# An FFT mixer and a routed expert layer on one core: two small expert blocks taken from the first half of the first batch

## The chip, the cores and the metric

The kernel runs on one core of a Trainium2 chip. The core has a matrix engine (TensorE, "PE" in the profile, with its weight loads "PEld"), a vector engine (VectorE, "DVE"), an activation engine (ScalarE, "ACT"), a general engine (GpSimd, "POOL") and SyncE ("SP"), which here only issues DMAs. Each engine works through its own instructions strictly in the order in which the program lists them, and waits for others by semaphores. Sixteen DMA engines move data between the core's memory and DRAM. The metric is the device time of one execution in microseconds.

## The reference

The input `x` is 8 batches of 2496 rows of 256 numbers. A two-dimensional Fourier transform is taken of each batch, and its real part is kept. The 19968 rows are then routed: each row goes to one of eight experts, the one with the largest logit.

```python
X = np.fft.fft(x, axis=1)
X = np.fft.fft(X, axis=2)
x = X.real.astype(np.float32).reshape(B * S, D)
logits = x @ w_gate
expert_idx = np.argmax(logits, axis=1)
...
for e in range(E):
    h = np.maximum(x_sorted[lo:hi] @ w1[e], 0.0)
    y_sorted[lo:hi] = h @ w2[e]
return gate_w[:, None] * y
```

`w1[e]` is 256x1024 and `w2[e]` is 1024x256, so a row costs an expert 524,288 multiplications; the weights of an expert are 2 MB in float32.

## The kernel before

**The transform of a batch** has two stages. `first(b)` (line 325) loads the batch in three parts, folds them on VectorE (`fold`, lines 299 to 310), multiplies by `w1` tables (`half1`, PSUM name `s`) and stores the result to a DRAM tensor `Td`. `regroup` (line 351) loads it back in another arrangement as `t4`. `second(b)` (line 361) takes one group after the other: `turn_last` (matmul `pr`), `group` (matmul `p<-table,t`, copied by ScalarE to `zz`), and for each of ten windows of 128 positions the last matmul (`p<-table,zz`), which gives the rows and their eight logits together. The ten windows are two halves of five (`h` is 0 or 1; `HW` is 5). A window gives 2 x 128 rows, a position and its mirror image, so a half has `NSL` = 10 slots of 128 rows. 24 of the first half's rows are doubles that are thrown out: it has 1256 rows.

**The routing** is done once for each half: `route` (line 416) finds the expert of each row, counts with bf16 matmuls (`rk`) how many rows of the same expert came before, and computes each row's place in `Xs`, a DRAM tensor with a long region for every expert (line 450 to 453). `base` holds how far each region is filled. For batch 0, VectorE writes the places directly as integers to `pi` (line 453); for later batches it writes floats to `pf`.

**The scatter.** `route` appends ten entries to the queue `waiting`. Each call of `send` (line 462) takes one: for later batches ScalarE copies the slot's place to `due` and GpSimd casts it to an integer (line 469); then GpSimd issues an indirect DMA that writes 128 rows to their places in `Xs` (line 470, and 236 in the profile). Writes to `Xs` and reads of it are ordered by dependency groups that `sent` and `taken` declare (lines 241 to 249): a block that is taken in round `b` waits for all scatters up to batch `b`, and not for those of `b + 1`.

**Expert blocks.** `rounds` (line 130) plans how many blocks are taken after which batch. After batch `b`, the number of rows is known, but not how they are spread over the experts; if every expert may leave a remainder smaller than a block, a certain number of full blocks is there in any case, and only these are planned. Before the change that gives 2 blocks of 256 and 4 of 128 rows after batch 0, 4 of 256 after batch 1, 3 of 512 after batch 2, 5 of 512 after each of the later ones, and in the last round 7 of 256 and 21 of 128 in addition. Which expert each of the planned blocks belongs to and where its rows start is computed on VectorE by `plan` (line 478), some twenty small instructions on one partition, in five turns (it yields four times; the table `tabs[b, size, last]` exists after the fifth). Its tables have room for `MOST` = 21 blocks, and their instructions work on all 21 whatever the number `k` of blocks is. `gone` holds what the blocks planned so far have taken.

**A block** (`experts`, line 701) needs its rows (`fetch_rows`, line 526: SyncE reads the table, then issues four DMAs at line 534 and one at line 538), its weights (`fetch_weights`, line 541: two DMAs of 1024 KB at lines 544 and 546, into one of three buffers), a transpose on VectorE with a negation on ScalarE (`turn`, line 576), the first product `ph` with its ReLU evictions (line 792 to 798), the second product `py` (line 833) and an indirect DMA for each 128 rows of the output. `fetch_some` (line 722) asks for weights and rows of the next blocks, as far as their tables exist and their batch is in the set `whole`.

**The order of the work** is written out by generators. Ahead of the main loop, `second(0)` runs with `first(1)` interleaved, and one `send` after each of its turns (line 937 to 940); eight of batch 0's twenty scatters are called there, the other twelve in the main loop. The main loop (line 943) asks `experts` for one step of expert work at a time; each yields a weight and a flag. For every step the loop lets `side` do a number of turns: `ticks` x weight / (`EARLY` x `open_`), where `ticks` is 44 in the first round and `open_` is 32, the weight of that round's blocks. A step of weight 0 without the flag is worth one turn. `side` in the first round weaves `close(0)` (the plans of batch 0) turn by turn with batch 1's and the next transform. Before the first block, the loop makes turns until the first table exists (nine), sends everything that is still waiting when `experts` yields `0, True` (line 744, 956 to 960), and makes nine more turns (line 746) ahead of the first transpose.

Of the kernel before, what the change touches and what calls it, by code (L numbers as in the profile page):

```python
# [50 lines left out]
def bc(ap, axis, n):  # L51
    shape = list(ap.shape)
    shape.insert(axis, n)
    return ap[tuple([slice(None)] * axis + [None])].to_broadcast(shape)
# [72 lines left out]
    return {n: np.ascontiguousarray(v, dtype=np.float32) for n, v in c.items()}  # L127


def rounds():  # L130

    want = [((256, 2), (128, 4)), ((256, 4),)] + [((512, B),)] * (B - 2)
    plan, used = [], 0

    def full(done, size):
        return max(0, -(-(done - used - E * (size - 1)) // size))

    for b in range(B):  # L140
# [12 lines left out]
        plan.append(now)  # L153
    return plan

SURE = -(-(NT - sum(size * k for now in rounds() for size, k, last in now if not last)) // REST)


def in_order():


    todo = []
    for b, now in enumerate(rounds()):
        parts = [[(b, size, last, i) for i in range(k)] for size, k, last in now]
        if b == B - 1:
            few, many = parts[-2:]
            sure, more = many[:SURE], many[SURE:]
            k = len(few)  # L170
# [45 lines left out]
def kernel(ctx: ExitStack, tc, x, w_gate, w1, w2, out):  # L216
# [52 lines left out]
    con, k = {}, 0  # L269
# [91 lines left out]
    def second(b):  # L361

        t4 = None

        def turn_last(h):

            nonlocal t4
            t4 = ahead.pop((b, "t4", h))
            n = min(HALF, NG - h * HALF)
            pr = pm_.tile([GP, HALF], F32, tag="m", name="pr")  # L370
            mm(pr[:, 0:n], con["rot"][:], t4[0:GP, 0:n, H])
            act.copy(t4[0:GP, 0:n, H], pr[:, 0:n])

        def group(g):
            i, n = g % HALF, LAST if g == NG - 1 else GP
            p2 = pm_.tile([128, 2, n], F32, tag="m", name="p2")
            for c in range(2):
                mm(p2[:, c], t4[0:GP, i, c * H:(c + 1) * H], con["m2"][:, c, 0:n])
            act.copy(zz[:, :, g * GP:g * GP + n], p2[:])  # L379
            if g == HALF - 1:  # L380
                turn_last(1)

        def mirror(rows, k):
            act.copy(free(rows[:], (k + 1) * W + D - 1, [-W, 2], [-1, H - 1]),
                     free(rows[:], k * W + 1, [W, 2], [1, H - 1]))

        turn_last(0)
        yield
        group(0)
        yield  # L390
        group(1)
        yield
        for h in range(2):
            rows = sp.tile([128, NSL, W], F32, tag="rows", name="rows")
            lg = sp.tile([128, NSL, E], F32, tag="lg", name="lg")
            for i in range(HW):
                w, k = HW * h + i, 2 * i
                if w + 2 < NG:
                    group(w + 2)
                p3 = pm_.tile([128, 2 * NY + 2 * E + 1], F32, tag="m", name="p3")  # L400
                z = zz[:, :, 128 * w:128 * (w + 1)]
                mm(p3[:, 0:NY + 2 * E], z[:, 0], con["rd"][:, 0, 0:NY + 2 * E], True, False, skip_group_check=True)
                mm(p3[:, NY:], z[:, 1], con["rd"][:, 1], False, True, skip_group_check=True)
                zs = sp.tile([128, NY + 1], F32, tag="zs", name="zs")
                act.copy(zs[:], p3[:, NY + 2 * E:])  # L405
                if i:
                    mirror(rows, k - 2)
                vec.tensor_copy(lg[:, k:k + 2], p3[:, NY:NY + 2 * E].rearrange("p (m e) -> p m e", m=2))  # L408
                for m, op in enumerate((ALU.add, ALU.subtract)):
                    vec.scalar_tensor_tensor(rows[:, k + m, 0:NY], p3[:, 0:NY], zs[:, 0:1], zs[:, 1:],  # L410
                                             op0=ALU.add, op1=op)
                yield
            mirror(rows, k)
            yield from route(b, h, rows, lg)

    def route(b, h, rows, lg):
# [33 lines left out]
        vec.tensor_tensor(pos[:], rk[:, 0:NSL], bc(base[:], 1, NSL), op=ALU.add)  # L450
        vec.tensor_tensor(pos[:], pos[:], oh[:, 0:NSL], op=ALU.mult)
        vec.reduce_sum(pf[:], pos[:], axis=AX_X)
        vec.tensor_tensor(pf[:] if b else pi[:], pf[:], con["far"][:, h], op=ALU.add)
        nxt = cp.tile([128, E], F32, tag="base", name="base", bufs=2)
        vec.tensor_tensor(nxt[:], rk[:, NSL], base[:], op=ALU.add)
        base = nxt
        for s in range(NSL):
            waiting.append((b, pf[:, s:s + 1], pi[:, s:s + 1], rows[:, s]))

    waiting = deque()  # L460

    def send():

        if waiting:
            b, place, idx, rows = waiting.popleft()
            if b:
                due = sp.tile([128, 1], F32, tag="due", name="due", bufs=8)
                act.copy(due[:], place)  # L468
                pool.tensor_copy(idx, due[:])  # L469
            sent(put_row(Xs, idx, rows, E * CAP - 1, "xs"), b)  # L470


# [5 lines left out]
    def plan(b, size, k, last):  # L478
# [3 lines left out]
        def one(name, *dims, dt=F32):  # L482
            return cp.tile([1, *dims], dt, tag="p_" + name, name="p_" + name, bufs=2)
# [10 lines left out]
        vec.tensor_tensor(ex[:], ce[:], nb[:], op=ALU.subtract)  # L494
        yield
        vec.scalar_tensor_tensor(rb[:], ex[:], -float(size), gone[:], op0=ALU.mult, op1=ALU.add)
        ge, ei = one("ge", MOST, E), one("ei", MOST)
        val, eq, rw = one("val", MOST, E + 1), one("eq", MOST, E + 1), one("rw", MOST)
        vec.tensor_tensor(ge[:], bc(bk["i"], 2, E), bc(ce[:], 1, MOST), op=ALU.is_ge)
        vec.reduce_sum(ei[:], ge[:], axis=AX_X)  # L500
        yield
        vec.tensor_tensor(eq[:], bc(ei[:], 2, E + 1), bc(bk["e9"], 1, MOST), op=ALU.is_equal)
        vec.memset(val[:, :, E:E + 1], float(E * CAP))
        vec.scalar_tensor_tensor(val[:, :, 0:E], bc(bk["i"], 2, E), float(size), bc(rb[:], 1, MOST),
                                 op0=ALU.mult, op1=ALU.add)
        yield
        vec.tensor_tensor(val[:], val[:], eq[:], op=ALU.mult)
        vec.reduce_sum(rw[:], val[:], axis=AX_X)
        tab = cp.tile([1, 2, MOST], I32, tag="p_tab", name="p_tab", bufs=4)
        vec.tensor_copy(tab[:, 0], rw[:])  # L510
        vec.tensor_scalar(tab[:, 1], ei[:], E - 1.0, None, op0=ALU.min)
        if last:
            cnt = cp.tile([1, 1], I32, name="cnt")
            vec.tensor_copy(cnt[:], ce[:, E - 1:E])
# [186 lines left out]
    def experts(todo):  # L701
# [35 lines left out]
        for k, (b, size, last, at) in enumerate(todo):  # L737
            n, m = size // 128, BIG // size
            if not k:
                while todo[0][:3] not in tabs:  # L740
                    yield 0, False
                fetch_some(0, 1)
                while b not in whole:
                    yield 0, True
                fetch_some(0)
                for _ in range(9):
                    yield 0, False
                for xT in turn(b, size, xbs[0][0]):
                    pass
# [114 lines left out]

    def close(b):

        for size, k, last in rounds()[b]:
            yield from plan(b, size, k, last)

    def through(b):  # L870
# [5 lines left out]
    def ahead_of(b):  # L876

        yield from first(b)
        regroup(b, 0)
        regroup(b, 1)  # L880
# [43 lines left out]
    for c in range(2):  # L924
# [6 lines left out]
            vec.tensor_scalar(con["rd"][:, c, to + E:to + 2 * E], pg[:], con["sgn"][:], None, op0=ALU.mult)  # L931
        else:
            vec.tensor_copy(con["rd"][:, c, to + E:to + 2 * E], pg[:])
    early = ahead_of(1)
    for _ in range(7):
        next(early)
    for k, _ in enumerate(second(0)):
# [5 lines left out]
    for b in range(1, B):  # L943
# [3 lines left out]
        ticks = TICKS + AHEAD * (b == 1)  # L947
        if b == 1:
            side = woven(chain(close(0), through(0)), chain(early, side))
        blocks = [(size, k * size / BIG, halved(b - 1, size)) for size, k, _ in rounds()[b - 1]]  # L950
# [76 lines left out]
```

## Time and profile before

| | us |
|---|---|
| median of 3 runs | 1272.84 (1270.5 to 1274.08) |
| profiled execution | 1280.92 |
| its span, first to last instruction | 1279.1 |
| TensorE busy / mean granted clock | 1221.0 (95%) / 0.972 |
| VectorE, ScalarE, GpSimd busy | 700.4 (55%), 436.3 (34%), 398.3 (31%) |
| indirect DMA to `Xs`, GpSimd, mean of one | 1.02 |
| cast of 128 places on GpSimd, mean of one | 0.28 |

In the lists of the profile a line has the start, the duration, the engine, the source line, the operation and its tiles, then how often in a row, and in brackets how long the engine was idle before it and who ended that. Every float32 matmul of the program stands as two records (`x8` is four matmuls). Ends of matmuls are modelled. "remote" stands where the trace doesn't tell what ended a wait. Line 221 is the helper through which all matmuls go, line 236 that of all indirect DMAs.

### The profile page before, as it was taken

The page shows a single profiled execution, that of the slowest core. Times are in us where ns is not written, and L with a number is a line of the kernel's source. Part 1 is how long each engine was busy: PE and PEld are TensorE (multiplying, and loading weights), DVE is VectorE, ACT ScalarE, POOL GpSimd, SP SyncE. Part 2 cuts the span into 40 slices and gives each one's busy share as a digit, 9 for nine tenths or more (in the row PEclk, how much of TensorE's full clock was granted, in tenths as well). Part 3 has the DMA queues.
Part 4 walks back from the last instruction along what each step waited for, and adds up shares of the span by engine and source line. Part 5 has one row for each costly group of instructions (what it writes and reads, how often), then busy time and mean ns, then how long its engine had stood idle before and what let it go on. Part 6 is the DMA issues. An engine that isn't in the chain of part 4 may idle for free.

```text
span 1279.1 us, 21208 instructions
## 1 busy us (share of the span) xinstructions
PE 1221.0 (95%) x6905; PEld 1077.0 (84%) x6905; DVE 700.4 (55%) x1772; ACT 436.3 (34%) x1096; POOL 398.3 (31%) x495
## 2 busy tenths in 40 slices
PE   6768999999999999999999999999999999999996
PEld 4557898876788888888888888888889999999995
DVE  4455434343466655564556455674578774444662
ACT  1423332332243433434343343432333332222232
POOL 0235327145116311561116411461453321111112
PEclk6859999999999999999999999999999999999998
DMA  8859798765348553573336434443435238778786
GB/s 241 279 181 321 242 339 297 204 228 175 125 146 260 162 153 113 175 240 114 104 118 211 144 120 149 132 152 107 130 121 167 91 129 296 283 277 276 280 279 246
DMA packets 163211, 249.72 MB, mean 195 GB/s; under 512 B 118601, under 2 KB 130227, under 8 KB 143516
## 3 DMA queue, kind: packets, MB, share of 16 engines
q1 hardware_dynamic: 146327, 203.28, 50.0%
q0 software_dynamic: 15888, 42.14, 9.1%
q10 hardware_dynamic: 885, 2.94, 0.7%
q8 instruction: 56, 0.92, 0.3%
q14 instruction: 55, 0.45, 0.1%
HBM read 194.91 MB, written 54.83 MB: 195 GB/s over the span
## 4 chain that ended last, share of the span: by engine, by line
PE 87%; DMA 6%; DVE 3%; another core or an unknown queue 2%; issue 1%; ACT 1%; SPq 0%; POOL 0%; POOLq 0%; DVEq 0%; ACTq 0%
PE py L221 32%; PE ph L221 10%; PE c L221 10%; PE a L221 10%; PE p L221 6%; PE d L221 6%; PE b L221 5%; PE e L221 4%; PE s L221 3%; DMA xq<-in_x_dram 2%; DMA Td<-t 1%; DMA t<-Td 1%; DMA xb<-Xs 1%; PE rk L221 0%
## 5 line engine op out<-in xcount | busy, mean ns | idle before, releaser
L221 PE MATMUL py<-w_sb,hT 128*128 128x256 f32 x2016 | 454.9, 380 | 1.3 <-DVE hT L796 1.3
L221 PEld LDWEIGHTS py<-w_sb,hT 128*128 128x128 f32 x2016 | 377.6, 190 | 51.2 <-DVE hT L796 1.7
L236 POOL DMA_INDIRECT out_dram<-y,ro x163 | 160.4, 984 | 694.0 <-ACT y L837 482.6
L236 POOL DMA_INDIRECT Xs<-rows,pi x160 | 163.2, 1020 | 109.9 <-DVE rows L410 52.1
L221 PE MATMUL ph<-xT,w_sb 128*128 128x128 f32 (+2 forms) x992 | 171.3, 328 | 6.1 <-DVE hT L796 3.3
L221 PEld LDWEIGHTS ph<-xT,w_sb 128*128 128x128 f32 x992 | 135.5, 192 | 30.5 <-issue 17.9
L837 ACT ACTIVATE y<-py,xb 128x256 f32<-128x256 f32 x129 | 61.0, 473 | 239.5 <-PE py L221 213.0
L221 PE MATMUL a<-xT,w_sb 128*128 128x256 f32 (+1 forms) x512 | 117.5, 356 | 0.0
L621 DVE TENSOR_TENSOR u<-p,b 128x512 f32<-128x512 f32 x57 | 39.1, 687 | 124.2 <-PE b L221 95.0
L796 DVE TENSOR_SCALAR hT<-ph 128x512 f32<-128x512 f32 x43 | 29.7, 690 | 129.5 <-issue 79.2
L221 PEld LDWEIGHTS a<-xT,w_sb 128*128 128x128 f32 x512 | 89.5, 190 | 10.7 <-DVE xT L582 0.4
L408 DVE COPY lg<-p 128x16 f32<-128x16 f32 x80 | 13.9, 174 | 141.5 <-ACT zs L405 121.3
L631 ACT ACTIVATE hT<-a 128x512 f32<-128x512 f32 x57 | 34.0, 597 | 149.5 <-PE a L221 115.7
L585 ACT ACTIVATE xT<-xT 128x256 f32<-128x256 f32 (+1 forms) x94 | 36.4, 387 | 121.8 <-DVE xT L582 71.9
L221 PE MATMUL s<-xq,w 104*112 104x256 f32 (+2 forms) x208 | 62.6, 426 | 11.0 <-DVE xq L297 10.9
L221 PEld LDWEIGHTS p<-table,t 120*128 120x128 f32 x352 | 55.2, 206 | 15.0 <-ACT zz L379 5.5
L221 PE MATMUL p<-table,zz 128*128 128x145 f32 (+1 forms) x320 | 57.2, 304 | 7.6 <-ACT t L321 5.5
L221 PE MATMUL p<-table,t 120*128 120x120 f32 (+1 forms) x352 | 57.7, 291 | 6.1 <-ACT zz L379 4.1
L221 PE MATMUL c<-xT,ws 128*128 128x256 f32 (+1 forms) x256 | 59.5, 359 | 3.2 <-DVE hT L627 3.2
L469 POOL CAST pi<-due 128x1 int32<-128x1 f32 x140 | 39.5, 282 | 69.1 <-ACT due L468 68.7
L582 DVE STREAM_TRANSPOSE xT<-xb 128x512 f32<-128x512 f32 (+1 forms) x94 | 58.2, 625 | 4.3 <-DMA xb<-Xs 4.3
L798 ACT ACTIVATE hT<-ph 128x512 f32<-128x512 f32 x55 | 32.8, 597 | 80.2 <-PE ph L221 64.9
(146 smaller groups left out, 1798.1 us busy)
## 6 DMA issues: line engine op xcount, KB each, us to landing
w_sb<-in_moe_w_dram SPq DMA_DIRECT2D x132, 1024.0 KB
xq<-in_x_dram SPq DMA_DIRECT2D x24, 896.0 KB
xb<-Xs SPq DMA_DIRECT2D x112, 128.0 KB
Td<-t SPq DMA_DIRECT2D x18, 448.0 KB
t<-Td SPq DMA_DIRECT2D x8, 768.0 KB
t<-Td SPq DMA_DIRECT2D x8, 640.0 KB
xb<-Xs SPq DMA_DIRECT2D x52, 64.0 KB
xb<-Xs SPq DMA_DIRECT2D x100, 32.0 KB
```

Source lines behind the costliest of these rows:

```text
L221: nc.tensor.matmul(o, lhsT=lhsT, rhs=rhs, start=start, stop=stop, **kw)
L236: return unordered(pool.indirect_dma_start(out=dst, out_offset=bass.IndirectOffsetOnAxis(ap=idx, axis=0), in_=rows, in_offset=None, bounds ...
L408: vec.tensor_copy(lg[:, k:k + 2], p3[:, NY:NY + 2 * E].rearrange("p (m e) -> p m e", m=2))
L469: pool.tensor_copy(idx, due[:])
L582: vec.transpose(free(xT[:], 256 * h, [32, n // 32], [BIG, 2], [1, 32]), free(xb, 512 * h, [64, n // 32], [1, 2], [2, 32]))
L585: act.activation(odd, odd, ACTF.Copy, scale=-1.0)
L621: vec.tensor_tensor(u2[:], p1[:], b[:], op=add)
L631: act.activation(h11, a[:], ACTF.Relu)
L796: vec.tensor_scalar(o, ph[:], 0.0, None, op0=ALU.max)
L798: act.activation(o, ph[:], ACTF.Relu)
L837: act.activation(y[:], py[:], ACTF.Copy, scale=meta[:, i, 1:2])
```

## The change

A new first stage, called batch -1 and named `HEAD`, holds two blocks of 128 rows that can be planned after the first half of batch 0. `rounds` counts their 256 rows as taken, so that batch 0's own list becomes one block of 256 and four of 128; the other rounds' lists stay as they were.

- The plan of these blocks, `heads = close(-1)`, takes one turn ahead of each of the five windows of batch 0's second half.
- The ten places of batch 0's first half stand in `waiting` under -1, those of its second half under 0, so their scatters are in different dependency groups.
- Batch 0's places are floats too, and GpSimd casts each slot's (from `pf` directly, without the copy by ScalarE) ahead of its scatter.
- `plan`'s instructions from line 499 on work on the `k` blocks of the plan instead of 21.
- There are eight turns of other work ahead of the first block's transpose instead of nine; the nine turns until the first table exists fall away, since the first table is there when the main loop begins.
- The main loop's first round counts the head's weight: `open_` stays 32.

```diff
+HEAD = [(REST, -(-(2 * 128 * HW - NB - E * (REST - 1)) // REST), False)]
 def rounds():
-    plan, used = [], 0
+    plan, used = [], sum(size * k for size, k, _ in HEAD)
...
+def stage(b):
+    return HEAD if b < 0 else rounds()[b]
...
 def in_order():
-    for b, now in enumerate(rounds()):
+    for b in range(-1, B):
+        now = stage(b)
...
             for i in range(HW):
+                if h and not b:
+                    next(heads, None)
...
-        vec.tensor_tensor(pf[:] if b else pi[:], pf[:], con["far"][:, h], op=ALU.add)
+        vec.tensor_tensor(pf[:], pf[:], con["far"][:, h], op=ALU.add)
...
-            waiting.append((b, pf[:, s:s + 1], pi[:, s:s + 1], rows[:, s]))
+            waiting.append((b if b or h else -1, pf[:, s:s + 1], pi[:, s:s + 1], rows[:, s]))
...
-            if b:
+            if b > 0:
                 due = sp.tile([128, 1], F32, tag="due", name="due", bufs=8)
                 act.copy(due[:], place)
-                pool.tensor_copy(idx, due[:])
+                place = due[:]
+            pool.tensor_copy(idx, place)
             sent(put_row(Xs, idx, rows, E * CAP - 1, "xs"), b)
...
-        ge, ei = one("ge", MOST, E), one("ei", MOST)
-        val, eq, rw = one("val", MOST, E + 1), one("eq", MOST, E + 1), one("rw", MOST)
-        vec.tensor_tensor(ge[:], bc(bk["i"], 2, E), bc(ce[:], 1, MOST), op=ALU.is_ge)
-        vec.reduce_sum(ei[:], ge[:], axis=AX_X)
+        ge, val, eq = (one(name, MOST, E + 1)[:, 0:k] for name in ("ge", "val", "eq"))
+        ei, rw = (one(name, MOST)[:, 0:k] for name in ("ei", "rw"))
+        count = bk["i"][:, 0:k]
+        vec.tensor_tensor(ge[:, :, 0:E], bc(count, 2, E), bc(ce[:], 1, k), op=ALU.is_ge)
+        vec.reduce_sum(ei, ge[:, :, 0:E], axis=AX_X)
...
-                for _ in range(9):
+                for _ in range(8):
                     yield 0, False
...
     def close(b):
-        for size, k, last in rounds()[b]:
+        for size, k, last in stage(b):
             yield from plan(b, size, k, last)
...
-    early = ahead_of(1)
+    heads, early = close(-1), ahead_of(1)
...
-        blocks = [... for size, k, _ in rounds()[b - 1]]
+        blocks = [... for size, k, _ in (HEAD if b == 1 else []) + stage(b - 1)]
```

More of the change, by code (lines that the diff above doesn't have):

```diff
@@ L154, in rounds @@
     return plan
-SURE = -(-(NT - sum(size * k for now in rounds() for size, k, last in now if not last)) // REST)
+def stage(b):
+    return HEAD if b < 0 else rounds()[b]
+SURE = -(-(NT - sum(size * k for now in [HEAD, *rounds()] for size, k, last in now if not last)) // REST)
 def in_order():
     todo = []
-    for b, now in enumerate(rounds()):
+    for b in range(-1, B):
+        now = stage(b)
         parts = [[(b, size, last, i) for i in range(k)] for size, k, last in now]
@@ L496, in plan @@
         vec.scalar_tensor_tensor(rb[:], ex[:], -float(size), gone[:], op0=ALU.mult, op1=ALU.add)
-        ge, ei = one("ge", MOST, E), one("ei", MOST)
-        val, eq, rw = one("val", MOST, E + 1), one("eq", MOST, E + 1), one("rw", MOST)
-        vec.tensor_tensor(ge[:], bc(bk["i"], 2, E), bc(ce[:], 1, MOST), op=ALU.is_ge)
-        vec.reduce_sum(ei[:], ge[:], axis=AX_X)
+        ge, val, eq = (one(name, MOST, E + 1)[:, 0:k] for name in ("ge", "val", "eq"))
[3 more added lines that the diff above has]
+        vec.reduce_sum(ei, ge[:, :, 0:E], axis=AX_X)
         yield
-        vec.tensor_tensor(eq[:], bc(ei[:], 2, E + 1), bc(bk["e9"], 1, MOST), op=ALU.is_equal)
+        vec.tensor_tensor(eq, bc(ei, 2, E + 1), bc(bk["e9"], 1, k), op=ALU.is_equal)
         vec.memset(val[:, :, E:E + 1], float(E * CAP))
-        vec.scalar_tensor_tensor(val[:, :, 0:E], bc(bk["i"], 2, E), float(size), bc(rb[:], 1, MOST),
+        vec.scalar_tensor_tensor(val[:, :, 0:E], bc(count, 2, E), float(size), bc(rb[:], 1, k),
                                  op0=ALU.mult, op1=ALU.add)
         yield
-        vec.tensor_tensor(val[:], val[:], eq[:], op=ALU.mult)
-        vec.reduce_sum(rw[:], val[:], axis=AX_X)
+        vec.tensor_tensor(val, val, eq, op=ALU.mult)
+        vec.reduce_sum(rw, val, axis=AX_X)
         tab = cp.tile([1, 2, MOST], I32, tag="p_tab", name="p_tab", bufs=4)
-        vec.tensor_copy(tab[:, 0], rw[:])
-        vec.tensor_scalar(tab[:, 1], ei[:], E - 1.0, None, op0=ALU.min)
+        vec.tensor_copy(tab[:, 0, 0:k], rw)
+        vec.tensor_scalar(tab[:, 1, 0:k], ei, E - 1.0, None, op0=ALU.min)
         if last:
@@ L949 @@
             side = woven(chain(close(0), through(0)), chain(early, side))
-        blocks = [(size, k * size / BIG, halved(b - 1, size)) for size, k, _ in rounds()[b - 1]]
+        blocks = [(size, k * size / BIG, halved(b - 1, size)) for size, k, _ in (HEAD if b == 1 else []) + stage(b - 1)]
         total = sum(k * (15 if seven_ else 16) for _, k, seven_ in blocks)
```

## The prediction

> **What bounds the kernel now.** I read the page's slices first, then stretches of 5 us, then the timeline around the first expert block, then SyncE's waits. The slices:
>
> ```profile
> PE   6768999999999999999999999999999999999996
> ...
> PEclk6859999999999999999999999999999999999998
> DMA  8859798765348553573336434443435238778786
> ```
>
> A slice is 32 us. From the fifth one on TensorE has work in every tenth that the row can show, at full clock; a matmul block saved or added there is time saved or added, and nothing else is. The idle time lies in the first four slices, so the change must be judged between about 52 us (first scatter) and 140 us. Stretches of 5 us, with busy time, granted clock, DMA share and GB/s:
>
> ```profile
> 60.00:65.00 5.00, 1.88 (x7) 0.50 0.85 307
> 65.00:70.00 5.00, 1.48 (x7) 0.50 0.22 78
> 70.00:75.00 5.00, 3.69 (x11) 0.50 0.69 189
> 75.00:80.00 5.00, 1.21 (x4) 0.50 0.99 375
> 80.00:85.00 5.00, 3.07 (x13) 0.50 0.24 76
> 85.00:90.00 5.00, 3.25 (x15) 0.77 0.48 86
> 90.00:95.00 5.00, 4.99 (x19) 0.66 0.76 254
> ```
>
> For 30 us TensorE has batch 1's transform pieces alone, with gaps and at half clock. What it waits for is the end of batch 0's scatter and, behind it, the first block's rows:
>
> ```profile
> 52.53 1.11 POOL L236 DMA_INDIRECT Xs<-rows,pi  x1 [52.08 <-DVE rows L410]
> 53.94 0.97 POOL L236 DMA_INDIRECT Xs<-rows,pi  x1 [0.30 <-issue]
> ...
> 78.33 0.97 POOL L236 DMA_INDIRECT Xs<-rows,pi  x1 [0.31 <-issue]
> ...
> 83.46 1.92 SPq L534 DMA_DIRECT2D xb<-Xs  x4
> ...
> 90.01 3.16 PE L221 MATMUL ph<-xT,w_sb 128*128 128x256 f32 x8 [1.75 <-DVE ro L755]
> ```
>
> Twenty scatters leave GpSimd from 52.53 to 79.30; SyncE stands at line 534 until 83.46; the first expert matmul runs at 90.01.
>
> **How much TensorE loses there.** At full clock four records of `p<-table,t` take 0.43 us start to start, four of `p<-table,zz` 0.51, four of `s` 0.86. From 61.3 to 90 the timeline holds 24 + 16 + 8 of them and two `pr`s: 2.6 + 2.0 + 1.7 + 0.3 = 6.6 us of work in 30 us, 23.4 lost. From 90 to 105 there are four groups of the first block's `ph` (1.73 each, 6.9 us) and 5.8 us of transform: 2.3 lost. So 25.7 us are lost from 60 to 105, beside 6.9 us of expert work and 12.4 us of transform done.
>
> **The change, part by part.**
>
> *One 256 block becomes two of 128.* By the planner's arithmetic batch 0 had 2x256 + 4x128 rows in sure blocks; now it has 2x128 (from its first 1256 rows), 1x256, 4x128. All later rounds stay the same. The price on TensorE is read from the pure 128 blocks:
>
> ```profile
> 159.80 3.73 PE L221 MATMUL ph<-xT,w_sb 128*128 128x128 f32 x32
> 163.37 3.62 PE L221 MATMUL py<-w_sb,hT 128*128 128x256 f32 x16
> 166.83 3.73 PE L221 MATMUL ph<-xT,w_sb 128*128 128x128 f32 x32
> ```
>
> 166.83 - 159.80 = 7.03 us for a block, 14.06 for two. A 256 block is four `ph` groups of 1.73 and two `py` of 3.46, 13.83. So +0.24 us. Evictions (4), output scatters (2) and row bytes stay the same. SyncE gets two more table loads, two weight transfers of 1024 KB and five row transfers.
>
> *When the first block can start.* Its rows need only sends 1 to 10. A cast goes ahead of each: with casts, sends follow at 121.80, 123.26, 124.71, so 1.455 us against 1.275 (53.94 to 55.22). First send 52.53 + 0.20 cast + 0.28 gap = 53.0; the tenth 9 x 1.455 later, 66.1. The twentieth was issued at 78.33 and SyncE was released at 83.46, so 5.1 us to landing at most: 71.2. From SyncE's row transfer to the first matmul took 83.46 to 90.01, 6.5 us, but with nine filler turns and a 256 block in between; its own parts are 1.92 issue, 0.43 transpose, 0.31 negation, and about 1.8 of flight, an estimate from these gaps: 4.5. First matmul at 75.7 (74 to 78).
>
> *The filler is postponed.* Before, 18 turns of side work passed ahead of the first block, nine of them batch 1's; now 8, four of them batch 1's: three folds on VectorE and one `pr`. So TensorE has almost nothing from 62 to 75.7: 15.6 lost from 60. This is the bill for starting earlier; the postponed transform has to be done between the head blocks. A weighted turn of a block still draws 44 / (0.7 x 32) = 1.96 turns.
>
> *The head blocks' own losses.* Cold clock: before, TensorE came back to full clock 4.4 us after its first block started, half of which is 2.2 lost. Late completions: ScalarE waited for transform results long after the matmuls' modelled ends, while GpSimd sent without a break:
>
> ```profile
> ACT t L372 <- remote: 5.0, 1, 5.0
> ACT zz L379 <- remote: 4.8, 1, 4.8
> ACT zs L405 <- remote: 4.0, 1, 4.0
> ```
>
> These fell between 61 and 81, 13.8 us in 20; VectorE had 7.7 more at 120 to 132. GpSimd will send until about 83.5 (20 x 1.455 from 53.0, and 1.4 for two sends that took 1.77 and 1.57 instead of 0.97), so the head lies 7.8 us in this. From 0 (280 to 300 us, where sends are as dense and no such wait stands) to 5.4 (7.8 x 13.8 / 20). I take 3.
>
> *The sum.* Before lost 25.7; after loses 15.6 + 2.2 + 3.0, and does 0.24 more: 4.7 us gained. What is late next is the 256 block's rows: batch 0's last send ends at 83.5 and lands by 88.6, its rows are there by 93 to 97; the head blocks need 14.1 of their own and 11 of transform from 75.7, beyond 104. Hidden by 7 us or more.
>
> *The queues.* SyncE asks for the first head block's weights once the early table is there, about 59.5 instead of 71.19, then stands at the head's rows until 71 rather than at batch 0's until 83.46; behind it are only the second head block's rows and weights, asked for by 78 and landed by 85, needed at about 90. On GpSimd each send waits for its own cast, 20 x 0.18 = 3.6 us over all, inside the cover just named; without that cover it would be paid once.
>
> *The plans.* `heads` puts five turns of plan work on VectorE among the second half's windows: with the rows of the present plan (1.48 us from line 488 to 494, then pieces of about 0.8, 0.7 and 1.7) some 4 to 5 us at most beside 1.7 us of VectorE idling there. It delays the second half's places from 63.6 to about 66.5; send 11 would go at 67.5, so nothing is paid. Shorter plans save some 0.15 us in six VectorE instructions of each of eleven plans; TensorE covers both: 0.
>
> The Trainium skill, "TensorE: Matmul & The Clock Gate", Part 1: The HAM clock gate, says that an idle window of some 3.4 us halves the clock and as much steady work restores it. It speaks against the change, which leaves a longer gap ahead of the head; the rows of 0.50 from 60 on agree. By that page the cold start would cost 1.7 instead of 2.2, and the sum would be an estimated 5.2.
>
> "SBUF — State Buffer", SBUF: two separate sides, says that a VectorE instruction with two SBUF inputs and a GpSimd instruction that reads SBUF shut each other out. The two slow sends at 65.44 and 67.51 stand beside such folds (lines 306, 295), which agrees. The early plan's two-input steps among the first ten casts could by that page hold GpSimd up by an estimated 1.8 us, and the gain would be 2.9.
>
> **The rivals.**
>
> *The first rows come late (slower).* Place: SyncE at line 534. If the row transfer waits for all twenty sends, the last is issued at 82.1, lands at about 88.6, and the first matmul runs at 93 with the filler not done: lost 32.9 + 2.2 up to there against 25.7, so -9.6 with the extra work, 1282. Every microsecond that the head starts after 80.4 is a loss; from 84.2 on it can be measured. For it: weights asked for at 59.5 compete with sends 5 to 10 on a DMA row at 0.85. Against: the two halves are in different dependency groups, and the DMA engines stand at 0.22 from 65 to 70.
>
> *The added weights meet full DMA engines.* From 92 to 136 us they are 0.92 to 1.03 busy at 306 to 347 GB/s. 2.1 MB more at 300 are 7 us; if paid there: 1272.8 - 4.7 + 7 = 1275.1. Against: the head's first weights fall into 60 to 70, the second's into 78 to 92, where the engines are at 0.22 to 0.5.
>
> *Late completions hold both head blocks*, at 5.4 for the first and a like stall of 2 for the second: 1272.8 - 0.3 = 1272.5, no change.
>
> *A better one.* No late completions (+3), and the stall of 120 to 132 (7.3 us: 1.99 us groups at 121.09 and 126.37 with 5.3 between) half gone: about 1261.
>
> **How the numbers follow.** The profiled execution took 1280.92, its span 1279.1, and is 8.1 above the median; the gain is a difference within it and is carried to the median: 1272.84 - 4.7 = 1268.1. About 0.3%, 3.8 us, is what a measurement of this kernel can tell from none. Chances: forecast 0.46 (two thirds below 1269.0), better 0.14, late completions 0.12, DMA 0.10, late rows 0.18. Faster 0.14 + 0.31 + 0.05 from the others' good ends = 0.50; slower: late rows and 0.03 of the DMA case, 0.21; the rest 0.29. The range goes from the better case, 1260, to near the late rows, 1279; the forecast's own is 1264 to 1272.
>
> **What would show it.** First `ph` of 128x128 near 76 and the second head block done near 105; the first row transfer at SyncE near 71; sends 1.46 us apart, the last near 83; no wait of TensorE for weights or rows of the 256 block; from 140 on the same picture, 4 to 5 us earlier. It is wrong if the row transfer stands until 83 or later, or if the stretch from 105 to 140 loses more than its 9 us.

## The result, and the profile after

| | before | after |
|---|---|---|
| median | 1272.55 us (1269.2 to 1278.6, 21 runs) | 1275.60 us (1272.88 to 1278.81, 21 runs) |
| ratio | | 1.0021, 95% interval 1.0012 to 1.0031 |
| profiled execution, its span | 1280.92, 1279.1 | 1274.43, 1272.6 |
| matmul records of the profile | 6905 | 6937 |

The changed kernel is 0.2% slower: within the 0.3% that counts as no change here, and not the 4.7 us (0.4%) less of the forecast. The two profiled executions say the opposite (6.5 us less). The one of before lies 8 us above its kernel's median and above all 21 of its runs, so single profiles are compared here only where they agree with others of the same kernel.

The lines after are other ones: 229 is the helper of the matmuls (221 before), 244 that of the indirect DMAs (236), 546 and 550 the row DMAs (534, 538), 556 and 558 the weights (544, 546), 350 the store to `Td` (342), 297 the load of `x` (289).

The slices of the page, 32 us each (busy tenths of TensorE, granted clock, DMA share):

```profile
PE   5758999999999999999999999999999999999996
PEclk9978999999999999999999999999999999999998
DMA  8878998765348543573336434443335238788786
```

The first four busy tenths were 6, 7, 6 and 8 before, and the clocks 6, 8, 5 and 9. In the third slice (64 to 96 us) TensorE works at a higher clock now, in the fourth (96 to 127) at a lower one. The same kernel in stretches of 5 us (columns: busy time and instructions of PE, PEld, DVE, ACT, POOL, then granted clock, DMA share, GB/s):

```profile
65.00:70.00 5.00, 0.00 (x0) 0.00 (x0) 3.25 (x17) 0.00 (x0) 4.17 (x7) 0.50 1.00 413
...
75.00:80.00 5.00, 2.95 (x14) 2.95 (x15) 1.66 (x9) 0.31 (x1) 3.99 (x8) 0.50 0.49 120
80.00:85.00 5.00, 5.00 (x30) 4.86 (x30) 1.53 (x2) 0.95 (x2) 3.32 (x5) 0.76 0.92 278
...
100.00:105.00 5.00, 2.97 (x14) 2.33 (x13) 1.07 (x3) 0.00 (x0) 0.00 (x0) 1.00 0.68 133
105.00:110.00 5.00, 1.82 (x17) 1.82 (x17) 3.79 (x15) 1.93 (x6) 0.97 (x1) 0.63 0.47 143
```

TensorE works from 77 at a clock that soon is full, as forecast. But from 103 to 108 it has nothing, at a place where before it had no gap (the same count `rk` in the timeline of before):

```profile
99.16 0.21 PE L221 MATMUL rk<-oh,tri 128*128 128x88 bf16 x1 [0.20 <-DVE oh L431]
```

The timeline of after shows that the head itself went as predicted (first and tenth send, first row transfer, first head matmul, last send):

```profile
53.83 1.13 POOL L244 DMA_INDIRECT Xs<-rows,pi  x1 [0.78 <-ACT zz L387]
...
68.49 0.98 POOL L244 DMA_INDIRECT Xs<-rows,pi  x1 [0.28 <-POOL pi L480]
...
72.69 1.92 SPq L546 DMA_DIRECT2D xb<-Xs  x4
...
77.05 6.38 PE L229 MATMUL ph<-xT,w_sb 128*128 128x128 f32 x32 [13.22 <-DVE ro L767]
...
83.00 0.98 POOL L244 DMA_INDIRECT Xs<-rows,pi  x1 [0.28 <-POOL pi L480]
```

What came instead stands in SyncE's own timeline after that (two weight transfers of the 256 block, a store, a load of `x`, the 256 block's rows) and in SyncE's waits from 50 to 115:

```profile
81.31 0.34 SPq L556 DMA_DIRECT2D w_sb<-in_moe_w_dram  x1
81.82 0.49 SPq L558 DMA_DIRECT2D w_sb<-in_moe_w_dram  x1
95.41 0.34 SPq L350 DMA_DIRECT2D Td<-t  x1
95.86 0.37 SPq L297 DMA_DIRECT2D xq<-in_x_dram  x1
98.25 1.90 SPq L546 DMA_DIRECT2D xb<-Xs  x4
```

```profile
SPq L350 <- ACT t L329: 13.0, 1, 13.0
```

SyncE stands 13.0 us at the store of a piece of batch 2's transform, whose last part ScalarE copies at 94.80 only. The rows of the 256 block, whose last scatter left at 83.00, are behind it in the queue and are asked for at 98.25. On TensorE and on VectorE that looks like this (timeline of after):

```profile
101.94 1.03 PE L229 MATMUL s<-xq,w 104*112 104x256 f32 x4
...
106.00 0.71 DVE L594 STREAM_TRANSPOSE xT<-xb 128x512 f32<-128x512 f32 x1 [4.92 <-DMA xb<-Xs]
...
107.89 0.24 DVE L441 TENSOR_TENSOR oh<-table,v 128x80 bf16<-128x80 f32 x1
...
108.18 0.23 PE L229 MATMUL rk<-oh,tri 128*128 128x88 bf16 x1 [5.21 <-DVE oh L441]
...
110.62 1.92 PE L229 MATMUL s<-xq,w 104*112 104x256 f32 x4
112.33 2.29 PE L229 MATMUL ph<-xT,w_sb 128*128 128x256 f32 x8
```

VectorE waits 4.92 us at the block's transpose for its rows. Behind that, in VectorE's order, stands batch 1's one-hot (line 441), and TensorE's next instruction, the count `rk`, waits for it 5.21 us. All transform work that could have filled the hole is behind `rk` in TensorE's order. The clock had fallen again by then: the `s` group takes 1.92 at 110.62 against 1.03 at 101.94. (The Trainium skill, "TensorE: Matmul & The Clock Gate", Part 1: The HAM clock gate, has an idle window of some 3.4 us halve the clock. That agrees: TensorE idles 5.2 us here, and the granted clock of 105 to 110 is 0.63.)

To compare kernels, I count each matmul record at the start-to-start time of its shape at full clock (0.216 us for 128x256 in float32) and subtract the sum from the length of a stretch: what is left is TensorE time lost. The figures depend a little on these prices, by up to some 0.6 us, but all rows alike.

| profile | lost 60 to 100 | 100 to 110 | 60 to 110 | 110 to 150 |
|---|---|---|---|---|
| before | 26.2 | 0.8 | 27.0 | 8.5 |
| before again (e0, e6) | 24.2, 26.5 | 0.5, 0.8 | 24.7, 27.3 | 8.5, 10.6 |
| after | 20.7 | 6.3 | 27.0 | 4.1 |
| after again (e5, e11) | 19.8, 17.9 | 7.0, 7.6 | 26.8, 25.5 | 8.3, 2.6 |
| rows early (e1, e10) | 21.1, 19.6 | 0.8, 0.9 | 21.9, 20.5 | 7.4, 2.7 |
| filler back (e2) | 17.1 | 0.3 | 17.4 | 14.2 |
| both (e4) | 18.2 | 0.3 | 18.5 | 13.6 |
| casts alone, before (e3) | 27.9 | 1.0 | 28.9 | 8.8 |
| head without casts (e7) | 19.8 | 6.9 | 26.7 | 12.0 |
| full plans (e8) | 17.9 | 6.7 | 24.6 | 3.0 |
| spaced sends, before (e9) | 25.3 | 0.4 | 25.7 | 3.4 |

Up to 100 the change gains 5.5 us in the first pair of profiles, and from 100 to 110 it gives 5.5 back; the other profiles of the two kernels show the same pattern.

### The profile page after: what moved, and what is told of

Its sections match the earlier page's. It is cut to its first block, busy times and chain, and to the rows that moved or that the text cites. A ratio compares the mean times of both kernels' runs of the same rounds, so it can differ in the third digit from the quotient of the medians.

```text
span 1272.6 us, 21363 instructions
## 1 busy us (share of the span) xinstructions
PE 1217.2 (96%) x6937; PEld 1080.6 (85%) x6937; DVE 696.2 (55%) x1794; ACT 436.4 (34%) x1097; POOL 405.7 (32%) x515
## 4 chain that ended last, share of the span: by engine, by line
PE 85%; DMA 6%; DVE 3%; POOL 2%; issue 2%; ACT 1%; SPq 1%; POOLq 0%; DVEq 0%; ACTq 0%
PE py L229 32%; PE ph L229 10%; PE c L229 10%; PE a L229 10%; PE d L229 6%; PE p L229 5%; PE b L229 5%; PE e L229 4%; PE s L229 3%; POOL Xs L244 1%; DMA t<-Td 1%; DMA xq<-in_x_dram 1%; DMA Td<-t 1%; DMA xb<-Xs 1%; DMA Xs<-rows,pi 1%
## 5 line engine op out<-in xcount | busy, mean ns | idle before, releaser
L229 PE MATMUL ph<-xT,w_sb 128*128 128x128 f32 (+2 forms) x1024 | 174.4, 327 | 13.2 <-DVE ro L767 13.2
L229 PEld LDWEIGHTS ph<-xT,w_sb 128*128 128x128 f32 x1024 | 140.7, 196 | 35.9 <-issue 16.5
L229 PEld LDWEIGHTS a<-xT,w_sb 128*128 128x128 f32 x512 | 89.8, 191 | 10.1
L418 DVE COPY lg<-p 128x16 f32<-128x16 f32 x80 | 13.8, 173 | 134.3 <-ACT zs L415 134.3
L229 PE MATMUL e<-xs,w_sb 128*128 128x256 f32 (+1 forms) x256 | 58.8, 357 | 0.0
L229 PE MATMUL d<-xT,w_sb 128*128 128x256 f32 (+1 forms) x256 | 58.7, 357 | 0.0
L229 PE MATMUL c<-xs,ws 128*128 128x256 f32 (+1 forms) x256 | 58.7, 357 | 0.0
```

What stands on the lines that cost most here:

```text
L229: nc.tensor.matmul(o, lhsT=lhsT, rhs=rhs, start=start, stop=stop, **kw)
```

## The experiments

Theory A, in the expectations: the gain was made and then lost because the 256 block's rows stood in SyncE's queue behind the store to `Td`. The other letters are rivals that the expectations put in words: the added weights, the postponed filler, a difference of chips. "Late completions" are waits of ScalarE or VectorE to read a matmul's result that the trace ends with `remote` only, long after the modelled end of the matmul; that the result itself came late is a reading, which no run here shows. Kernels compared in one set ran on one chip; the chips of the first two sets took 1286.5 and 1284.5 us for the kernel before, instead of 1272.6 and 1273.3, so only ratios are carried across.

### First set: before 1286.46 us (23 runs)

**Before again**, unedited, to see which waits of its profile come back.

> The unchanged kernel, profiled a second time. Theory A (the late rows of the 256 block ate the gain): the first profiled execution of before, 1280.9 us, was 8 us above the median of its runs, and held a stall of some 7 us at 120 to 132 us that a usual execution does not have. Then this profile shows a time near 1273, TensorE's first expert matmul again near 90 us, and less than 3 us of idle TensorE between 120 and 136 us, where the first one had 5.7. Theory B (the head simply gains nothing because TensorE's work between 60 and 90 us was already useful): the stall at 120 to 132 us is a fixed part of the kernel and is seen again, 5 to 7 us.

Measured 1279.5, one run. The first expert matmul and what ScalarE waited for from 61 to 81 (timeline and waits of e0):

```profile
89.42 2.01 PE L221 MATMUL ph<-xT,w_sb 128*128 128x256 f32 x8 [1.75 <-DVE ro L755]
```

```profile
ACT zz L379 <- remote: 5.3, 2, 4.1
ACT t L372 <- remote: 5.0, 1, 5.0
```

Late first rows and late completions both come back, and so does the stall at 120 to 132: TensorE waits 1.8 us at 122.64 and 2.1 at 129.32 for `hT`. So the expectation that a usual execution lacks this stall and takes near 1273 missed. The 24 to 27 us lost up to 110 stand in all three profiles of before (e6 is the third), and the starting point of the forecast stood on that; no execution at the median of the faster chips was profiled.

**Rows early.** The kernel after, with the 256 block's rows asked for ahead of the second head block's step of `fetch_some`:

```diff
+            if b < 0 and at:
+                while todo[k + 1][:3] not in tabs:
+                    yield 0, False
+                while todo[k + 1][0] not in whole:
+                    yield 0, True
             fetch_some(k)
```

> The changed kernel, but the 256 block's rows are asked for before the second head block's first product instead of after it, so that SyncE's row transfer stands ahead of batch 2's store to Td in its queue. Theory A (the change loses 8 us at 102 to 112 us because SyncE stood 13.0 us at that store, with the row transfer behind it): the row transfer starts by 89 us instead of 98.25, the idle time of TensorE at 102 to 108 us is gone, and the time falls by 5 to 9 us, to 1267 to 1271. Theory C (the added 2.1 MB of weights in full DMA engines make the rows late, wherever they stand in the queue): the rows still land after 102 us and the time stays within 2 us of the changed kernel's 1275.6.

1277.99 us (12 runs), ratio 0.9951 [0.9931, 0.9970]. SyncE in its timeline:

```profile
90.50 1.97 SPq L546 DMA_DIRECT2D xb<-Xs  x4
92.67 0.40 SPq L550 DMA_DIRECT2D xb<-Xs  x1
95.86 0.33 SPq L350 DMA_DIRECT2D Td<-t  x1
```

The rows are asked for 7.75 us earlier (90.50; by 89 was expected), when SyncE's wait of 5.9 us for the scatter ends, and ahead of the store, which goes about when it went anyway (95.86). The loss from 100 to 110 is 0.8. Nothing about casts, weights or bytes was touched. The unedited kernel after did not run in this set; the third set puts the two side by side.

**Filler back.** Sixteen turns of other work ahead of the first head block instead of eight:

```diff
-                for _ in range(8):
+                for _ in range(16):
```

> The changed kernel with sixteen turns of other work ahead of the first head block instead of eight, so that eight turns, four of them batch 1's, move back into the 13.2 us in which TensorE idles from 63.8 to 77.05 us. Theory D (what the change loses is the transform that was postponed behind the head blocks): the time falls by 2 to 4 us, to 1271.6 to 1273.6, with the first head matmul still near 77 us. Theory A: the head starts at 77 to 79 us, the turns done early bring batch 2's store to Td forward as well, so the row transfer moves a little, and the time changes by no more than 2 us either way unless that store moves ahead of 90 us.

1276.73 us (6 runs), 0.9941 [0.9921, 0.9961]. The head did not start later, and SyncE did not stand at the store either (timeline of e2; the first line is cut off at 80 us, where its view ends):

```profile
77.17 3.14 PE L229 MATMUL ph<-xT,w_sb 128*128 128x128 f32 x13 [7.41 <-DVE rows L420]
...
84.18 0.35 SPq L350 DMA_DIRECT2D Td<-t  x1
84.63 0.47 SPq L297 DMA_DIRECT2D xq<-in_x_dram  x1
90.46 2.40 SPq L546 DMA_DIRECT2D xb<-Xs  x4
...
131.42 0.56 PE L229 MATMUL pr<-t,table 120*120 120x6 f32 x2 [7.30 <-DMA t<-Td]
```

With more of the transform done before the head, the store is ready at 84.18 instead of 95.41, and the row transfer moves to 90.46, where e1 had it. This is a second way to the same time of asking, and to about the same gain. It is less clean than e1, since it also moves TensorE's work: its profile loses 4 us less than e1's up to 100, and then 14.2 from 110 to 150, 7.30 of it waiting for a transform's second stage to come back from `Td`.

**Casts alone**, the kernel before with GpSimd casting batch 0's places:

```diff
-        vec.tensor_tensor(pf[:] if b else pi[:], pf[:], con["far"][:, h], op=ALU.add)
+        vec.tensor_tensor(pf[:], pf[:], con["far"][:, h], op=ALU.add)
...
-                pool.tensor_copy(idx, due[:])
+                place = due[:]
+            pool.tensor_copy(idx, place)
```

> The kernel before with one part of the change alone: batch 0's places are floats and GpSimd casts each slot's ahead of its scatter. Twenty casts put 20 x 0.18 = 3.6 us on GpSimd before batch 0's last scatter, and here, unlike in the changed kernel, nothing but this scatter releases the first block. If the scatter's end sets the first block's start, that block starts 3 to 4 us later than 90 us and the time rises by 2 to 4 us, to 1274.5 to 1276.5. If it is the filler turns ahead of the block that set it, the time stays within 1 us of 1272.6.

1288.28 us (12 runs), 1.0015 [0.9998, 1.0033]. SyncE and TensorE in the timeline of e3:

```profile
86.83 1.92 SPq L535 DMA_DIRECT2D xb<-Xs  x4
...
91.36 3.78 PE L221 MATMUL ph<-xT,w_sb 128*128 128x256 f32 x8 [12.54 <-DVE ro L756]
```

The longer scatter makes the first rows 2.9 us later than in e0 (83.94) and the first matmul 1.9 later; the time is 1.8 us longer, with an interval from none to 4.2. Both lie between the two outcomes expected. No wait from 61 to 81 ends on a late completion here.

### Second set: before 1284.51 us (23 runs)

**Both edits.**

> The changed kernel with both edits: the 256 block's rows asked for before the second head block, and sixteen turns of other work ahead of the first head block. Theory A (late rows) and theory D (postponed filler) name different idle times, 102 to 112 us and 63.8 to 77 us, so they should add: with both, less than 3 us of TensorE are lost from 90 to 120 us, and the time lies 6 to 10 us below the changed kernel's in the same comparison. If one edit only moves the wait of the other, it lies within 2 us of the better of the two alone, which were 0.9951 and 0.9941 of before.

1277.19 us (6 runs), 0.9944 [0.9926, 0.9961]. The rows are asked for at 91.50. The time is 8.3 us below that of the kernel after on this chip (next run) and within 2 us of either edit alone, so both outcomes that the expectation set against each other came true; the ratios (0.9951 and 0.9941 for one edit) show that the edits do not add up. From 100 to 110 either edit alone leaves 0.3 to 0.9 us lost, so the other finds nothing there. What the filler gains up to 100 (18.2 lost, against 21.1 and 19.6 in e1 and e10) goes again from 110 to 150 (13.6), with TensorE waiting 4.9 us at 131.66 for `Td`. Whether the two would add up without that wait was not tried.

**After again**, unedited.

> The changed kernel itself, unedited, beside its own variants. The kernel before took 1286.5 us in the last comparison and 1272.6 in the first, so only kernels that ran side by side can be told apart. Theory A: the changed kernel has the loss of 8 us at 102 to 112 us again, and its ratio to before is above those of the two variants (0.9951, 0.9941) by 0.003 to 0.007: 0.997 to 1.002. Theory E (the kernel before is what differs between comparisons: where it is slow, it has late matmul completions at 61 to 81 us, which the changed kernel does not have): the ratio is 0.993 to 0.997 where before takes 1286, and 1.002 where it takes 1272, with the changed kernel itself at 1274 to 1279 in both.

1285.44 us (12 runs), 1.0011 [0.9996, 1.0026]. SyncE waits 11.8 us at the store and asks for the rows at 97.45; TensorE idles 5.83 us ahead of `rk`. The hole is no accident of one execution. It also ends the rival that after takes one time on every chip and only before varies: after takes 10 us more here than in the first comparison.

**Before a third time.**

> The unchanged kernel, profiled a third time, to see what goes with its time. Theory E: if its time is near 1272, the ScalarE waits at 61 to 81 us and the VectorE waits at 120 to 132 us that end with late matmul completions (13.8 and 7.7 us in the first profile, 12.7 and 6.0 in the second) are smaller by 8 us or more; if it is near 1280 or above they are there again.

1286.12 us, one run, with late completions in both places, as expected for a time above 1280 (4.1 us at 61 to 81, 14.7 at 110 to 145).

**Head without casts**, the kernel after with batch 0's places written as integers by VectorE (the diff of e3 the other way round).

> The changed kernel with one part undone: VectorE writes batch 0's places as integers, as before, and GpSimd casts none of batch 0's twenty slots. The ten casts ahead of the head's last scatter take 1.8 us, so the head's first product moves from 77 to about 75 us. If the head's start sets the time, it falls by 1.5 to 2 us against the changed kernel; by theory A it stays within 1 us, because SyncE's queue and not the scatter sets when the 256 block's rows come. If the casts are what keeps late matmul completions away at 61 to 81 us (the casts alone in the kernel before showed none there), such waits come back, and the time rises.

1286.85 us (11 runs), 1.0018 [0.9998, 1.0038]. First head matmul (its line cut off at 80 us too) and SyncE in the timeline of e7, and below it two of the waits from 61 to 81:

```profile
75.45 4.76 PE L229 MATMUL ph<-xT,w_sb 128*128 128x128 f32 x21 [12.96 <-issue]
...
94.65 0.35 SPq L350 DMA_DIRECT2D Td<-t  x1
95.10 0.37 SPq L297 DMA_DIRECT2D xq<-in_x_dram  x1
97.49 2.30 SPq L545 DMA_DIRECT2D xb<-Xs  x4
```

```profile
ACT t L380 <- remote: 5.7, 1, 5.7
...
DVE pos L460 <- remote: 5.0, 1, 5.0
```

The head starts 1.6 us earlier than in the after profile and 1.2 earlier than in e5 on this chip (76.64), and the 256 block's rows are asked for at 97.49, as in e5 (97.45). The time is 1.4 us above that of e5, a little more than the 1 us that was expected, but within both intervals. So an earlier head showed no gain while SyncE stands at the store, and the casts are not what cost it. The late completions at 61 to 81 came back without the casts, as the last sentence of the expectation has it.

### Third set: before 1273.34 us (23 runs)

**After beside**, unedited, and **rows early again** on the same chip.

> The unedited kernel after, as what the two others beside it are held against. Ratio to the kernel before 1.000 to 1.003; SyncE stands 11 to 13 us at batch 2's Td store and TensorE idles about 5 us ahead of the 256 block's counts.

> The kernel after, with the 256 block's rows asked for ahead of the second head block's second product, a second time, now beside the unedited kernel after on one chip. Theory A: 6 to 9 us less than the unedited one, ratio to the kernel before 0.993 to 0.997. If the difference between the two was one of chips: within 2 us of the unedited one.

After: 1275.46 us (12 runs), 1.0013 [1.0004, 1.0023]. Rows early: 1268.72 us (6 runs), 0.9954 [0.9939, 0.9969]: 6.7 us less beside each other, and 4.6 less than before, where the forecast had 4.7. The edit is that of the first set, so the rows are asked for ahead of the second head block's first product. SyncE's store and row transfer and TensorE's counts in the timeline of e11:

```profile
92.64 0.34 SPq L350 DMA_DIRECT2D Td<-t  x1
...
95.47 2.30 SPq L546 DMA_DIRECT2D xb<-Xs  x4
...
105.62 0.23 PE L229 MATMUL rk<-oh,tri 128*128 128x88 bf16 x1 [5.42 <-DVE oh L441]
```

and in e10:

```profile
89.77 1.90 SPq L546 DMA_DIRECT2D xb<-Xs  x4
...
94.40 0.33 SPq L350 DMA_DIRECT2D Td<-t  x1
...
102.20 0.20 PE L229 MATMUL rk<-oh,tri 128*128 128x88 bf16 x1 [0.25 <-DVE oh L441]
```

In the two traces TensorE, VectorE, ScalarE and GpSimd work through the same instructions in the same order from start to end. The only difference in what is issued is on SyncE: one store to `Td` and one load of `x` stand behind the five transfers of the 256 block's rows instead of ahead of them. The lost time up to 110 goes from 25.5 to 20.5 us, 5.0 of the 6.7; where the other 1.7 sit is not settled. Theory A is shown by this, and the edit makes a kernel that is about 0.5% faster than both others.

**Full plans**, the kernel after with the plans' instructions on 21 blocks again.

> The kernel after, with the plans' instructions on 21 blocks again. Theory A (a block's rows behind SyncE's wait at the Td store is what ate the gain): nothing changes, its ratio to the kernel before lies within 0.002 of that of the unedited kernel after beside it, which I expect at 1.000 to 1.003. A theory in which the shorter plans carry part of the time: slower by 1.5 us or more, 0.0012 above the unedited one; the plan of the head's two blocks then takes about 2 us more on VectorE among the second half's windows, and the second half's scatters go later than 68 us.

1275.02 us (12 runs), 1.0009 [0.9996, 1.0022], against 1.0013 for the unedited kernel beside it: the shorter plans are worth nothing that can be measured, and the last send goes at 82.30, so they did not make room for the head either.

**Spaced sends**, the kernel before with a copy of nothing to do with the places ahead of each of batch 0's sends:

```diff
+            else:
+                idle = sp.tile([128, 1], I32, tag="idle", name="idle", bufs=8)
+                pool.tensor_copy(idle[:], con["lane"][:])
             sent(put_row(Xs, idx, rows, E * CAP - 1, "xs"), b)
```

> The kernel before, with an unrelated 128-place copy on GpSimd ahead of each of batch 0's sends; the places still come from VectorE as integers. Sends then follow about 1.45 us apart instead of 1.275. If the spacing of the sends is what keeps the late completions of matmuls away from 61 to 81 us, none of ScalarE's waits there ends on an event that the trace doesn't tell (with casts alone: 0 us of them; without: 12 us and more). If it is who writes the places, they are there as before, 12 us or more in that stretch. Time as before within 0.3% in either case.

1277.08 us, one run. The sends in e9's timeline:

```profile
58.02 0.98 POOL L236 DMA_INDIRECT Xs<-rows,pi  x1 [0.16 <-issue]
59.01 0.20 POOL L472 CAST idle<-table 128x1 int32<-128x1 f32 x1
59.36 0.98 POOL L236 DMA_INDIRECT Xs<-rows,pi  x1 [0.16 <-issue]
```

They mostly follow 1.34 us apart, not the 1.45 expected (the send doesn't wait for this copy: 0.16 us lie between them, and 0.28 where the copy makes the send's places), and no late completion stands from 61 to 81. That speaks for the gap between sends and against the writer of the places; but no kernel with unspaced sends was profiled on this chip, so it stays a hint. The loss up to 110 is 25.7, that of before.

## Why the prediction was wrong

*Right: the work and the head.* The profile of after has 64 records of 128x128 in place of 32 of 128x256; at 0.112 and 0.216 us each that is 0.26 us more work (0.24 forecast). The last send is at 83.00 (near 83), the first row transfer at 72.69 (71.2), the first head matmul at 77.05 (75.7, range 74 to 78). The tenth send went at 68.49 instead of 66.1: the first left 0.83 us later than counted, one, at 65.93, took 2.08 us instead of 0.98, and two casts took 0.3 us more than usual. From there to the row transfer were 4.2 us instead of 5.1, which gave part of it back. The long send ran beside VectorE's folds of 0.67 us at 65.87 and 66.47, which the forecast had named with "SBUF — State Buffer", SBUF: two separate sides, of the Trainium skill, without counting it in its sum; e9 repeats it (a GpSimd cast of 1.06 instead of 0.20 at 63.96, beside folds from 63.70).

*Right in sum, by other parts: "15.6 + 2.2 + 3.0".* From 60 to 100 the after profile lost 20.7 us; the forecast's terms add up to 20.8. The gap ahead of the head was 16.8 instead of 15.6 (60 to 77.05, all but about 0.3 of work), and the cold first group 6.38 against 3.73 at full clock, 2.65 instead of 2.2. The "I take 3" for late completions was wrong: with casts between the sends there was none to speak of (1.1 us at most in the five kernels with casts that ran in the first two sets), and the remaining 1.3 are small gaps up to 100.

*Wrong: "What is late next is the 256 block's rows: ... its rows are there by 93 to 97 ... Hidden by 7 us or more."* This is the step that failed. When the scatter ended was nearly right: 88.6 was counted, and asked for ahead of the store, the rows go at 89.8 to 90.5 (e10, e1). But they were asked for at 98.25 and used at 106.00. The working counted DMA flights and forgot the queue on which the transfer had to stand. The sentence on the queues said that behind SyncE's wait "are only the second head block's rows and weights"; that is true of the wait at the head's rows, and was not asked of the next. In the kernel before, the rows of both 256 blocks are issued before the store: the first at 83.46, then, in the timeline of before,

```profile
86.76 2.29 SPq L534 DMA_DIRECT2D xb<-Xs  x4
...
91.45 0.37 SPq L342 DMA_DIRECT2D Td<-t  x1
```

After, the order has turned round: the store and a load of `x` come between the head's transfers and the 256 block's.

*And why that store is late* stands in the prediction's own paragraph "the filler is postponed". It costed the postponement as TensorE time ahead of the head. The postponed turns are also those that make the piece which the store takes; once head blocks stand between them, its last `s` group is at 93.65, ScalarE's copy at 94.80, the store at 95.41. e2, which puts the turns back, has it at 84.18. One postponement was so paid twice: once before the head, and 5.2 us with a cold clock behind it at 102 to 113.

*The rivals.* Late first rows did not happen (72.69, not 83 or later). The added weights did not show: the rows of e1 and e10 came in time beside the same weights, and TensorE waits for no weight in the stretch. That this rival's time, 1275.1, is half a microsecond from the measured 1275.60 is chance: beside the same weights e10 takes 6.7 us less than e11. Late completions did not hold the head. None of the rivals named the 256 block's transfer, which had been put aside as hidden. Nor did the signs of being wrong point there: the row transfer of the head did not stand until 83, and from 105 to 140 the after profile loses about 7 us, not more than 9; the hole begins at 103.

*Open.* The lost time up to 110 is about the same before and after (24.7 to 27.3 against 25.5 to 27.0), which fits times that are about equal. The medians of the three comparisons have after 0.9 to 3.1 us above before. Where these sit is not settled: from 110 to 150 single profiles of one kernel differ by 5.7 us.

## What to carry to other kernels

When a transfer is called hidden, read the queue that issues it, and not only its data: on a queue that works in order, everything that the program lists ahead of it has to be ready too, here a store that waited for another engine's copy. Filler that is moved past a block takes its products along: ask which store, load or count the postponed work feeds, and who stands behind that. When two edits give the same gain each and no more together, they may have removed the same wait, or a new one may have come behind it, as partly here: read the stretch. An edit that only moves one transfer in one queue, with all else in the same order, says more on the cause.

## What the runs showed of the hardware

*Scatters beside folds.* It is the start that counts. Of the sends between 50 and 100 us in all fourteen profiles, 23 began while VectorE ran a fold of two SBUF inputs (0.6 to 1.2 us each), and 22 of these took 1.13 to 2.09 us, ending some 0.9 us after the folds. The one at 65.93 is one of them: the folds end at 67.14, the send at 68.02. 21 others began ahead of a fold that started beside them, and 20 of these took 0.97 to 0.99, as the one at 64.28 in the after profile, with a fold of 1.21 from 64.40.

*Late completions.* On the two slower chips ScalarE and VectorE waited for matmul results 4.1 to 13.4 us in all from 61 to 81 in every profile in which GpSimd sent batch 0's rows without a cast between them (e0, e6, e7), and 1.1 us at most with casts (e1 to e5). On the chip of the first comparison the profile of before had 13.8 us of them, and that of after none. What ends these waits the trace does not tell. These waits cost little here, since TensorE waited for rows at the same time: e7 and e5 lose 26.7 and 26.8 up to 110.

*A second place.* From 105 to 150 such waits stand in all eight profiles of those two chips (2.5 to 14.7 us) and in the first profile of before (7.7), and in none of the four profiles of the third set, nor in the first of after. Losses from 110 to 150 go with them: 2.6 to 3.4 in the third set, 7.4 to 14.2 on the slower chips, though not profile by profile: e2 has the smallest such wait (2.5) and the largest loss. Whether they are what makes those chips 1% slower was not tried, and what causes them is open.
